# A state-space layer and a SwiGLU block on one core: another order of the 1050 steps behind the first 150, and other engines for some roundings

## The chip, the cores and the metric

The kernel runs on one core of a Trainium2 chip. Its engines work from queues of their own and wait for one another by semaphores: TensorE (PE) multiplies matrices into PSUM, VectorE (DVE), ScalarE (ACT) and GpSimd (POOL) work elementwise, and SyncE (SP) issues most of the DMA transfers. The metric is the device time of one execution in microseconds.

## The reference, cut to what matters

The first half is a chunked scan with a state for each of 4 batches and 8 heads (768 positions, 32 values a head, 16 states), the second an RMS norm and a SwiGLU block on the 3072 rows of 256 that come out of it.

```python
for c in range(nc):
    la = log_a[:, :, sl]
    cum = np.cumsum(la, axis=-1)
    L = np.exp(cum[:, :, :, None] - cum[:, :, None, :]) * causal
    M = np.einsum('bhin,bhjn->bhij', Cc, Bc) * L
    y_intra = np.einsum('bhij,bhjd->bhid', M, xc)
    y_inter = np.einsum('bhin,bhnd->bhid', Cc, state) * np.exp(cum)[:, :, :, None]
    y[:, :, sl] = y_intra + y_inter
    decay_from_j = np.exp(cum[:, :, -1:] - cum)
    Bx = np.einsum('bhjn,bhjd->bhjnd', Bc, xc) * decay_from_j[:, :, :, None, None]
    state = np.exp(np.sum(la, axis=-1))[:, :, None, None] * state + np.sum(Bx, axis=2)
...
xn = x / np.sqrt(np.mean(x * x, axis=-1, keepdims=True) + 1e-06) * rms_g
g = xn @ w_gate
silu = g * (1.0 / (1.0 + np.exp(-g)))
return (silu * (xn @ w_val) @ w_out)
```

## The kernel before

The tokens are worked through in 6 blocks of 512. For each block the scan makes decay matrices L (spread by a DMA, `spread` L653; `subtract` L659; a causal cut L631; an exponential on ACT, L272), products g of C and B (L765), the states' additions A (L830) and the outputs y (L916). From y come the squares (ACT, added by `squares_added` L974 on DVE or POOL), their means ms on PE (L1014), the roots (L272, a load, and a DMA at L1032 and L1039) and the normed rows. The second half of a block has 12 groups f of 128 hidden values, each with a gate and a value product (index m), and 12 output products of two halves.

Large products in float32 are done in three fp32r products of parts: a rounded high part, a low part and a mixed part. So xh, xl, xk stand for the block's rows, wh, wp for the weights, hh, hl, hk for the hidden values. `gv_split` (L1159, step X) is one such product of 6 matmuls; `gv_whole` (L1149, step F) and `products_early` (L1112) are the plain float32 form for block 0. `silu_gv` (L272, ACT) takes the gate product out of PSUM, `hide_gv` (L1174, DVE) multiplies it with the value product into hx, `hid_high` rounds it to hh on ACT (`by_scalar`, L328, step hH) or on DVE (`by_vector`, L331, step hHv), and `hid_part` makes hl on DVE or POOL (L1080, steps hL and hLp) and hk on DVE (L1082). Output products are `product_o` (L1228 in blocks 1 to 4; L1234 for blocks 0 and 5, steps OF and OX) and `product_apart` (L1206, step OY) for the last two quarters of block 5. Results leave by `put` (L1258, L1264) and `put_apart` (L1216).

The weights come in 18 pieces k, fetched by SP (L238, L241, step fetch.k) into a buffer of their own each. ACT (step pow) and DVE (man, wt) turn a piece into float32 values w; wH (ACT) or wHv (DVE) make the high part, wL and wM (L322, DVE) the two others.

Two functions of ACT need different tables: silu, and the set with exponentials and logarithms. `functions` (L264 and L266) issues a table load wherever the next function in the order needs the other table.

What sets the order is a string of 1200 steps, written out by hand: each step calls one of the functions above, and so issues its instructions on each engine and on SP behind those of the steps ahead of it. An engine executes its own share in that order. Buffers are taken first-free from rings in the order of the steps: eight PSUM banks, 29 buffers of 512 float32 for parts and hidden values, and some others.

Of the kernel before, what the change touches and what calls it, by code (L numbers as in the profile page):

```python
# [50 lines left out]
def kernel(  # L51
# [1264 lines left out]
    def token_out():  # L1316
# [92 lines left out]
        i:fetch.9 i:fetch.7 i:fetch.14 b:F.0.4.0 p:S.3 b:xHv.0.1 i:wt.12 p:yi.2 i:man.10 p:ya.2
        p:yi.3 b:silu.0.5 i:man.8 i:wt.10 p:ya.3 i:pow.7 i:man.7 b:silu.0.4 i:hid.0 p:qc.4  # L1410
        p:spread.11 i:wHv.3 i:fetch.15 i:wt.7 i:pow.8 b:F.0.4.1 b:OF.0.1.0 b:silu.0.3 b:sq.1.1
        i:wHv.10 b:yt.1.1 b:xL.0.0 i:wM.3 i:fetch.11 b:yt.1.0 p:spread.10 b:OF.0.0.1 i:wt.8 b:xL.0.1
        b:OF.0.0.0 i:wL.10 i:wM.10 b:xK.0.1 p:spread.9 b:OF.0.1.1 b:sq.1.0 i:wH.7 b:F.0.5.1 i:wL.7
        p:qc.5 i:wM.7 b:X.0.11.0 b:sqa.1 i:wL.3 i:pow.14 b:hid.0.4 b:X.0.7.1 i:wHv.8 i:fetch.13
        b:X.0.2.1 i:man.15 i:wH.5 i:man.14 b:table.5 b:hid.0.7 b:X.0.3.1 b:ms.1 i:fetch.17 p:qb.4
        i:pow.11 i:pow.15 i:wM.8 i:man.11 i:wL.8 b:X.0.6.1 b:rs.1 b:hid.0.3 p:subp.10 b:X.0.9.0
        b:hid.0.5 b:X.0.8.0 i:pow.13 i:wt.11 i:wt.14 b:hid.0.6 i:pow.9 i:man.9 i:wt.15 i:man.13
        i:pow.17 p:sub.9 i:wHv.11 b:hid.0.2 i:wM.11 i:wt.9 i:wL.11 p:vB.4 p:ex.9 b:OF.0.4.0 i:man.17
        i:wH.9 i:wH.15 p:vC.4 b:OF.0.4.1 i:wt.13 b:OF.0.7.1 i:wL.9 i:wH.13 p:spread.8 b:OF.0.5.1
        i:wM.9 p:Tt.4.0 p:subp.11 p:qb.5 p:vC.5 b:rb.1 p:ex.11 b:X.0.10.0 p:x.4 i:wt.17 p:sub.8  # L1420
        b:OF.0.7.0 b:xn.1.1 p:qb.7 b:silu.0.11 p:scale.5 i:wH.4 i:wHv.1 b:xn.1.0 i:wHv.0 b:silu.0.9
        b:X.0.11.1 b:OF.0.5.0 b:xH.1.1 i:wH.17 i:wM.6 p:dT.5 i:wM.0 b:silu.0.8 b:OF.0.2.0 b:OF.0.3.1
        b:xH.1.0 b:xK.1.1 b:silu.0.10 b:X.0.9.1 i:fetch.16 b:OF.0.3.0 i:wL.0 p:dT.4 p:ca.9 b:X.0.8.1
        p:Tt.4.1 b:xL.1.0 p:ex.8 p:Tt.5.1 b:X.0.10.1 b:xK.1.0 i:pow.16 b:xL.1.1 b:exps.1 i:man.16
        b:hid.0.10 p:vB.5 b:OF.0.6.1 b:OF.0.2.1 p:qc.7 b:hid.0.11 b:X.1.0.0 p:ex.10 i:wt.16
        b:OF.0.6.0 p:ca.11 b:X.1.10.0 p:Tt.5.0 b:X.1.10.1 b:OF.0.11.1 i:wL.6 p:x.6 b:hid.0.8 p:qc.6
        b:hid.0.9 p:vB.7 b:silu.1.0 p:Td.4 b:silu.1.10 p:ca.8 b:gb.2 p:dT.6 i:wH.14 b:OF.0.8.1
        i:wM.2 b:X.1.9.0 p:ca.10 p:x.5 b:OF.0.10.1 i:wL.1 b:L.2.2 b:OF.0.9.1 b:L.2.0 b:X.1.8.0
        p:scale.4 i:wH.16 i:wM.15 p:Td.5 b:silu.1.9 p:A.5 b:L.2.3 i:wM.17 p:qc.9 b:L.2.1 p:vC.6
        p:vC.7 p:A.4 p:S.4 p:S.5 i:wH.12 p:Tt.7.1 b:OF.0.9.0 i:wL.17 p:x.7 b:X.1.0.1 b:put.0.1  # L1430
        b:OF.0.8.0 b:hid.1.0 p:yi.4 p:ya.4 p:Tt.6.1 i:wM.1 p:yi.5 p:ya.5 b:hid.1.10 i:wL.12 b:hH.1.0
        i:wM.12 b:silu.1.8 i:wM.4 b:X.1.11.0 b:hH.1.10 b:yt.2.1 b:OF.0.10.0 p:spread.14 p:qb.6
        b:OF.0.11.0 p:scale.7 p:vC.9 i:wL.4 p:scale.6 p:Tt.6.0 b:silu.1.11 b:X.1.1.0 b:table.4
        b:sq.2.1 b:put.0.0 b:hK.1.10 b:X.1.6.0 p:Tt.9.0 b:X.1.11.1 i:wL.15 b:hLp.1.0 i:wM.16
        b:X.1.6.1 b:silu.1.1 b:sq.2.0 b:hK.1.0 b:sqav.2 p:vB.6 p:dT.7 p:spread.12 b:yt.2.0 i:wM.5
        p:spread.13 b:ms.2 b:silu.1.6 i:wM.13 p:A.6 i:wL.16 p:spread.15 p:A.7 p:S.6 b:X.1.5.0
        i:wL.13 b:rs.2 b:hid.1.11 p:Tt.7.0 p:qb.10 i:wL.5 p:scale.9 p:S.7 b:exps.4 b:silu.1.5
        b:X.1.9.1 p:sub.13 b:X.1.1.1 b:X.1.4.0 b:X.1.8.1 b:exps.5 b:rb.2 b:hH.1.11 b:silu.1.4
        p:ex.13 p:Td.6 b:X.1.2.0 b:hid.1.1 b:hid.1.6 b:hK.1.11 p:sub.15 p:sub.14 b:xn.2.1 b:X.1.4.1
        b:X.1.3.0 b:hL.1.11 p:Tt.9.1 b:X.1.5.1 b:silu.1.2 b:hL.1.10 b:X.1.2.1 b:OX.1.0.1 p:subp.12  # L1440
        b:hid.1.4 b:silu.1.3 p:ex.14 b:hid.1.9 p:Td.7 b:hid.1.8 i:wM.14 b:OX.1.11.1 b:hid.1.5
        p:ex.12 b:hH.1.8 p:qb.9 p:ex.15 b:gb.3 p:qc.11 p:cav.14 b:OX.1.11.0 p:ca.15 p:qc.8 b:hid.1.2
        b:hH.1.1 p:cav.12 p:cav.13 b:OX.1.10.1 b:xn.2.0 b:L.3.2 b:OX.1.0.0 b:OX.1.10.0 b:L.3.1
        b:hH.1.6 b:X.1.7.0 b:hLp.1.8 b:L.3.3 b:silu.1.7 p:yi.6 b:L.3.0 b:hK.1.8 p:ya.6 b:xH.2.1
        b:X.1.7.1 b:xH.2.0 b:OX.1.8.0 i:wL.14 b:X.1.3.1 b:hHv.1.4 p:yi.7 p:ya.7 p:vB.9 b:xK.2.0
        b:hK.1.1 b:xL.2.0 b:xL.2.1 b:hid.1.3 b:hH.1.2 b:hLp.1.1 b:xK.2.1 b:hLp.1.4 b:hid.1.7
        b:yt.3.0 b:hK.1.4 b:OX.1.8.1 b:hHv.1.9 b:hLp.1.6 b:X.2.2.0 b:hH.1.7 b:OX.1.1.0 p:spread.16
        b:sq.3.1 b:OX.1.4.1 b:hK.1.9 b:OX.1.4.0 b:sq.3.0 p:spread.18 p:vC.8 b:OX.1.1.1 p:x.9
        b:yt.3.1 p:dT.8 b:hL.1.2 b:hLp.1.7 b:X.2.9.0 b:sqav.3 b:hL.1.9 p:qb.8 b:X.2.0.1 b:hK.1.7
        b:X.2.2.1 b:silu.2.2 p:Tt.8.0 b:silu.2.9 p:sub.16 p:scale.11 p:vB.8 b:X.2.11.0 b:OX.1.7.0  # L1450
        p:sub.18 b:OX.1.7.1 p:x.8 b:hH.1.3 b:hK.1.2 p:scale.8 b:OX.1.9.0 b:ms.3 p:A.8 b:OX.1.2.0
        b:hK.1.3 p:S.8 b:hid.2.2 p:spread.17 b:hL.1.3 p:vC.11 p:ex.16 p:subp.17 b:X.2.7.0 b:X.2.5.0
        b:silu.2.11 b:hHv.1.5 p:Tt.8.1 p:Td.8 b:hK.1.6 p:cav.16 p:spread.19 b:X.2.0.0 b:hL.1.5
        b:X.2.5.1 b:silu.2.0 b:OX.1.9.1 b:silu.2.5 p:vB.10 p:qc.10 b:OX.1.3.1 b:hid.2.5 b:rs.3
        p:dT.11 p:qb.11 b:hH.2.5 b:hid.2.0 p:ex.17 p:ex.18 b:X.2.8.0 p:subp.19 b:hK.1.5 p:ca.18
        p:Tt.11.1 b:X.2.11.1 p:dT.9 b:OX.1.6.1 b:hLp.2.5 p:ex.19 b:X.2.4.0 b:rb.3 b:OX.1.6.0
# [98 lines left out]
```

## Time and profile before

| | us |
|---|---|
| three runs | 364.86, 364.84, 364.15 (median 364.84) |
| profiled execution | 364.29 |
| its span in the trace | 362.5 |
| PE busy | 356.3 |
| DVE busy | 275.3 |
| ACT busy | 183.9, with 28 table loads of 1.283 |
| POOL busy | 74.8 |
| TensorE clock granted | 1.00 |

PE, DVE, ACT and POOL are the engines, PEld is the loading of weights into PE, which overlaps its matmuls. A float32 matmul of the program shows as two records in the trace, one with fp32r operands as one. A row of the chain or the timeline begins with the start and the duration in us; in brackets stands how long the engine had been idle ahead of it, and what released it. "issue" is time in which an engine waited for nothing that the profile shows.

### The profile page before, as it was taken

The page shows a single profiled execution, that of the slowest core. Times are in us where ns is not written, and L with a number is a line of the kernel's source. Part 1 is how long each engine was busy: PE and PEld are TensorE (multiplying, and loading weights), DVE is VectorE, ACT ScalarE, POOL GpSimd, SP SyncE. Part 2 cuts the span into 40 slices and gives each one's busy share as a digit, 9 for nine tenths or more (in the row PEclk, how much of TensorE's full clock was granted, in tenths as well). Part 3 has the DMA queues.
Part 4 walks back from the last instruction along what each step waited for, and adds up shares of the span by engine and source line. Part 5 has one row for each costly group of instructions (what it writes and reads, how often), then busy time and mean ns, then how long its engine had stood idle before and what let it go on. Part 6 is the DMA issues. An engine that isn't in the chain of part 4 may idle for free.

```text
span 362.5 us, 8200 instructions
## 1 busy us (share of the span) xinstructions
PE 356.3 (98%) x3301; PEld 284.0 (78%) x3301; DVE 275.3 (76%) x514; ACT 183.9 (51%) x323; POOL 74.8 (21%) x79
## 2 busy tenths in 40 slices
PE   8999989999999999999999999999999999999996
PEld 5667467888787888788788788788788888888886
DVE  6899998999999999872787884696457446629591
ACT  3879878697288946563236755225811121231110
POOL 4022004124011036212102626010010000511140
PEclk9999999999999999999999999999999999999999
DMA  8889968367525224423302031200101000100004
GB/s 103 187 140 288 272 193 224 107 151 117 103 85 137 44 40 103 103 54 85 60 12 81 7 88 31 45 0 4 36 0 31 1 0 2 29 0 2 0 7 110
DMA packets 94702, 27.95 MB, mean 77 GB/s; under 512 B 77545, under 2 KB 92617, under 8 KB 94665
## 3 DMA queue, kind: packets, MB, share of 16 engines
q1 hardware_dynamic: 92584, 27.30, 32.8%
q8 instruction: 26, 0.43, 0.5%
q10 hardware_dynamic: 2080, 0.13, 0.4%
q14 instruction: 12, 0.09, 0.1%
HBM read 23.68 MB, written 3.74 MB: 76 GB/s over the span
## 4 chain that ended last, share of the span: by engine, by line
PE 95%; DVE 2%; issue 1%; POOL 1%; ACT 0%; POOLq 0%; DVEq 0%
PE gv L1159 50%; PE o L1228 18%; PE o L1234 7%; PE gv L1149 4%; PE y L916 3%; PE o L1206 2%; PE gv L1112 2%; PE g L765 2%; PE A L830 1%; PE g L758 1%; PE y L891 1%; PE e L609 1%; POOL hl L1080 1%; PE ms L1014 0%; DVE hk L1082 0%
## 5 line engine op out<-in xcount | busy, mean ns | idle before, releaser
L1159 PE MATMUL gv<-xh,wh 128*128 128x512 f32 x264 | 84.8, 402 | 0.0
L1159 PE MATMUL gv<-xl,wp 128*128 128x512 f32 x264 | 81.5, 390 | 0.0
L1159 PE MATMUL gv<-xk,wp 128*128 128x512 f32 x264 | 81.4, 389 | 0.0
L272 ACT ACTIVATE hx<-gv 128x512 f32<-128x512 f32 x70 | 40.1, 595 | 75.3 <-PE gv L1159 36.5
L1080 POOL TENSOR_TENSOR hl<-hx,hh 128x512 fp32r<-128x512 f32 x27 | 39.5, 1473 | 172.4 <-PE o L1228 105.8
L1174 DVE SCALAR_TENSOR_TENSOR hx<-gv,hx 128x512 f32<-128x512 f32 x70 | 46.6, 683 | 26.9 <-PE gv L1159 19.3
L1159 PEld LDWEIGHTS gv<-xl,wp 128*128 128x128 f32 x264 | 49.6, 188 | 10.6
L1159 PEld LDWEIGHTS gv<-xk,wp 128*128 128x128 f32 x264 | 49.6, 188 | 10.6
L1159 PEld LDWEIGHTS gv<-xh,wh 128*128 128x128 f32 x264 | 48.6, 188 | 10.5 <-issue 0.6
L1082 DVE SCALAR_TENSOR_TENSOR hk<-hx,hh 128x512 fp32r<-128x512 f32 x60 | 47.1, 792 | 8.9 <-PE o L1228 6.0
L328 ACT ACTIVATE hh<-hx 128x512 fp32r<-128x512 f32 x35 | 21.8, 629 | 43.2 <-PE o L1228 20.3
L1228 PE MATMUL o<-hh,wh 128*128 128x512 f32 x96 | 38.0, 396 | 0.0
L1228 PE MATMUL o<-hl,wp 128*128 128x512 f32 x96 | 37.4, 390 | 0.0
L1228 PE MATMUL o<-hk,wp 128*128 128x512 f32 x96 | 37.4, 389 | 0.0
L1080 DVE TENSOR_TENSOR hl<-hx,hh 128x512 fp32r<-128x512 f32 x33 | 24.1, 744 | 5.3 <-PE o L1228 3.7
L631 POOL TENSOR_SCALAR_AFFINE_SELECT L<-L 64x512 f32<-64x512 f32 (+1 forms) x22 | 18.7, 851 | 45.8 <-ACT L L272 45.0
L322 DVE SCALAR_TENSOR_TENSOR wp<-wh,w 128x512 fp32r<-128x512 f32 x36 | 26.3, 756 | 1.0 <-ACT wh L328 1.0
L1234 PE MATMUL o<-w,hx 128*128 128x256 f32 x96 | 23.0, 381 | 0.0
L1228 PEld LDWEIGHTS o<-hh,wh 128*128 128x128 f32 x96 | 18.0, 188 | 4.3 <-issue 0.4
L1228 PEld LDWEIGHTS o<-hk,wp 128*128 128x128 f32 x96 | 18.0, 188 | 3.8
L1228 PEld LDWEIGHTS o<-hl,wp 128*128 128x128 f32 x96 | 18.0, 188 | 3.5
L1234 PEld LDWEIGHTS o<-w,hx 128*128 128x128 f32 x96 | 18.0, 189 | 3.4 <-issue 0.4
(180 smaller groups left out, 504.3 us busy)
## 6 DMA issues: line engine op xcount, KB each, us to landing
L<-rowd SPq DMA_DIRECT2D x32, 128.0 KB
x<-in_x_dram SPq DMA_DIRECT2D x24, 128.0 KB
...
```

Of the source, the lines that this page charges most:

```text
L272: nc.scalar.activation(**operands)
L322: nc.vector.scalar_tensor_tensor(out=(low_parts, mixed_parts)[i][k], in0=high_parts[k], scalar=(-UP, GAIN)[i], in1=view(ws[k], shape), op0 ...
L328: nc.scalar.activation(out=out, in_=in_, func=AF.Copy, scale=scale)
L631: nc.gpsimd.affine_select(out=L[r], in_=L[r], pattern=[[0, L.shape[1]], [1, HC]], compare_op=ALU.is_ge, fill=0.0, base=0, channel_multipli ...
L916: nc.tensor.matmul(out=o[first:first + n, (p % 2 * 2 + i) * HC:(p % 2 * 2 + i + 1) * HC], start=not groups & opened, stop=True, skip_group ...
L1080: engine.tensor_tensor(out=out, in0=v, in1=high, op=ALU.subtract)
L1082: nc.vector.scalar_tensor_tensor(out=out, in0=v, scalar=REST, in1=high, op0=ALU.mult, op1=ALU.subtract)
L1149: nc.tensor.matmul(out=o, lhsT=view(ws[k], fetched[k][2])[:, t, f % 2 * P:][:, 0:P], rhs=xn[:, t], start=(t == 0), stop=(t == 1))
L1159: nc.tensor.matmul(out=o, lhsT=weights_of(m, t, f)[part], rhs=view(x, [P, TB], F32R), start=(part == t == 0), stop=(part == 2 and t == 1))
L1174: nc.vector.scalar_tensor_tensor(out=v, in0=o, scalar=gain(blk, f), in1=v, op0=ALU.mult, op1=ALU.mult)
L1228: nc.tensor.matmul(out=o, lhsT=w[:, b * P:(b + 1) * P], rhs=v, start=opens, stop=True, skip_group_check=True)
L1234: nc.tensor.matmul(out=o[:, j * DM:(j + 1) * DM], lhsT=v[:, tk], rhs=w, start=opens, stop=True, skip_group_check=True)
```

## The change

Only the string of steps differs. Its first 150 steps and the number of steps are the same; behind them every piece of the string is in another order. A few steps are exchanged for others that do the same on another engine: of the hidden values' roundings hH goes from 35 to 29 and hHv from 25 to 31; of their low parts hL from 33 to 28 and hLp from 27 to 32; of the weights' high parts wH from 10 to 15 and wHv from 8 to 3; of the rows' high parts xH from 9 to 8 and xHv from 3 to 4; of the subtractions, those on DVE from 9 to 6 and those on POOL from 7 to 10; the additions of squares on DVE from 4 to 0 and on POOL from 1 to 5. Table loads follow from the order: 28 before, 38 now. PE's matmuls are the same in number and kind.

```diff
-        i:early.1.0 i:norm.0 p:Tt.2.0 p:T.3 p:Tt.3.1 i:wHv.2 b:xH.0.0 i:man.5 p:Tt.3.0 i:wL.2
...
+        i:early.1.0 i:norm.0 p:Tt.2.0 p:T.3 p:Tt.3.1 i:wHv.2 i:fetch.14 p:Tt.3.0 i:ca.2 p:scale.2
...
-        b:OY.2.0 b:put.4.1 b:OY.1.0 b:putv.5.0 b:puta.1 b:putva.0
...
+        b:put.4.1 b:putv.5.0 b:OY.2.1 b:OY.1.1 b:putva.0 b:puta.1
```

*The first block's outputs (35 to 50 us of the trace before).* PE's rows at that place, of the change against before; g, A and y are the scan's small products, L1112 and L1149 block 0's gate and value products.

```order
+L1112 MATMUL gv<-yt,w 128x256 x8
 L1149 MATMUL gv<-xn,w 128x512 x2
-L1112 MATMUL gv<-yt,w 128x256 x4
 L765 MATMUL g<-T 64x128 x32
 L1149 MATMUL gv<-xn,w 128x512 x6
 L830 MATMUL A<-x,Bd 32x64 x28
-L1149 MATMUL gv<-xn,w 128x512 x4
+L1149 MATMUL gv<-xn,w 128x512 x6
 L916 MATMUL y<-T,S 64x64 x16
 L916 MATMUL y<-L,x 32x64 x32
 L916 MATMUL y<-T,S 64x64 x12
```

Behind A now stand six L1149 matmuls ahead of the y group, where four stood; a group of four L1112 matmuls stands ahead of g, where it stood behind the first two L1149.

SP's transfers at the same time, first before, then with the change (wr are weight pieces, bc and bq rows of B and C, L the spread decays).

```order
L241 DMA wr_720<-in_moe_w_gate_dram 128x2x1023
L241 DMA wr_810<-in_moe_w_val_dram 128x2x1023
L241 DMA wr_812<-in_moe_w_val_dram 128x2x1023
L238 DMA wr_814<-in_moe_w_out_dram 128x2x1023
L173 DMA bc_944<-in_B_dram 128x8x16 x2
L186 DMA bc_944<-in_C_dram 128x1x128 x2
L653 DMA L_949<-rowd_98 64x512 x2
L238 DMA wr_954<-in_moe_w_out_dram 128x2x1023
L241 DMA wr_982<-in_moe_w_val_dram 128x2x1023
```

```order
L238 DMA wr_653<-in_moe_w_out_dram 128x2x1023
L241 DMA wr_717<-in_moe_w_val_dram 128x2x1023
L238 DMA wr_719<-in_moe_w_out_dram 128x2x1023
L241 DMA wr_721<-in_moe_w_val_dram 128x2x1023
L241 DMA wr_742<-in_moe_w_gate_dram 128x2x1023
L238 DMA wr_801<-in_moe_w_out_dram 128x2x1023
L241 DMA wr_925<-in_moe_w_val_dram 128x2x1023
L238 DMA wr_987<-in_moe_w_out_dram 128x2x1023
L653 DMA L_997<-rowd_98 64x512 x4
```

Eight weight pieces stand one behind the other where four stood; the rows of B and C, and the spreads, come behind them.

*The end of the program.* POOL's last instructions, before and with the change (the numbers are those of buffers' contents, so hl_4347 is the low part that is made from hx_4079).

```order
L1080 TENSOR_TENSOR hl_4161<-hx_3929,hh_4148 128x512
L1080 TENSOR_TENSOR hl_4220<-hx_3864,hh_4154 128x512
L1080 TENSOR_TENSOR hl_4300<-hx_4159,hh_4289 128x512
L1080 TENSOR_TENSOR hl_4317<-hx_4211,hh_4259 128x512
L1080 TENSOR_TENSOR hl_4347<-hx_4079,hh_4330 128x512
```

```order
L1080 TENSOR_TENSOR hl_4180<-hx_3990,hh_4084 128x512
L1080 TENSOR_TENSOR hl_4241<-hx_4093,hh_4218 128x512
L1080 TENSOR_TENSOR hl_4279<-hx_4016,hh_4239 128x512
L1080 TENSOR_TENSOR hl_4298<-hx_3906,hh_4151 128x512
L1080 TENSOR_TENSOR hl_4353<-hx_4293,hh_4300 128x512
```

PE's rows that wait for such parts, before and with the change (L1234 and L1206 are output products of block 5).

```order
L1234 MATMUL o_4095<-wh14_1390,hh_4289 128x256
L1234 MATMUL o_4095<-wp_1927,hl_4300 128x256
L1234 MATMUL o_4095<-wp_1927,hk_4308 128x256
L1234 MATMUL o_4095<-wh14_1390,hh_4289 128x256
L1234 MATMUL o_4095<-wp_1927,hl_4300 128x256
L1234 MATMUL o_4095<-wp_1927,hk_4308 128x256
L1206 MATMUL o_4102<-wh17_1224,hh_4259 128x256
L1206 MATMUL o_4102<-wp_1446,hl_4317 128x256
L1206 MATMUL o_4102<-wp_1446,hk_4277 128x256
```

```order
L1206 MATMUL o_4124<-wh14_1268,hh_4239 128x256
L1206 MATMUL o_4124<-wp_1683,hl_4279 128x256
L1206 MATMUL o_4124<-wp_1683,hk_4304 128x256
L1206 MATMUL o_4124<-wh13_1352,hh_4229 128x256
L1206 MATMUL o_4124<-wp_1588,hl_4326 128x256
L1206 MATMUL o_4124<-wp_1588,hk_4281 128x256
L1234 MATMUL o_4117<-wh12_1100,hh_4300 128x256
L1234 MATMUL o_4117<-wp_1187,hl_4353 128x256
L1234 MATMUL o_4117<-wp_1187,hk_4339 128x256
```

Before, PE takes hl_4300 and hl_4317 within these nine matmuls and hl_4347 another 25 behind them, all three of POOL's last instructions. Now hl_4353 alone is POOL's last, and what PE reads ahead of it here (hl_4328, hl_4279, hl_4326) it has had before.

*The middle, 145 to 175 us.* ACT's rows, before and with the change (L264 loads the table with silu, L266 the one with exponentials; hx<-gv is a silu, L<-L an exponential).

```order
L995 COPY yt<-y 64x4x64 x2
L272 ACTIVATE hx<-gv 128x512
L328 ACTIVATE T<-T,tmask 128x256
L272 ACTIVATE hx<-gv 128x512
L328 ACTIVATE hh<-hx 128x512
L266 ACT_TABLE_LOAD
L272 ACTIVATE L<-L 128x512
L264 ACT_TABLE_LOAD
L272 ACTIVATE hx<-gv 128x512
L328 ACTIVATE T<-T,tmask 128x256
L272 ACTIVATE hx<-gv 128x512 x2
L266 ACT_TABLE_LOAD
```

```order
L266 ACT_TABLE_LOAD
L272 ACTIVATE L<-L 128x512
L264 ACT_TABLE_LOAD
L272 ACTIVATE hx<-gv 128x512 x3
L266 ACT_TABLE_LOAD
L272 ACTIVATE L<-L 128x512 x2
L328 ACTIVATE T<-T,tmask 128x256
L264 ACT_TABLE_LOAD
L272 ACTIVATE hx<-gv 128x512
L266 ACT_TABLE_LOAD
L272 ACTIVATE roots<-ms,eps 128x128
L272 ACTIVATE roots<-roots 128x128
```

Before, three table loads stand in twelve rows, now five, and each silu of the stretch stands between two of them.

More of the change, by code (lines that the diff above doesn't have):

```diff
@@ L1409 @@
[L1409 to L1456, printed above, removed]
@@ new lines @@
+        b:silu.0.4 p:ya.3 b:sq.1.1 b:sq.1.0 i:wt.8 i:pow.11 i:pow.10 b:OF.0.0.0 i:wt.14 b:xK.0.1
+        i:wt.7 b:OF.0.0.1 b:F.0.5.1 i:fetch.17 i:hid.1 i:wH.7 b:OF.0.1.1 i:man.10 b:hid.0.4
+        p:spread.8 p:spread.10 p:qb.4 b:sqa.1 b:xL.0.0 b:ms.1 p:spread.9 b:xL.0.1 p:spread.11
+        b:yt.1.0 b:OF.0.1.0 b:OF.0.4.0 i:wH.8 i:wL.3 i:man.11 b:yt.1.1 i:fetch.13 b:rs.1 i:wt.10
+        b:X.0.3.1 i:wL.7 i:wM.7 b:X.0.2.1 i:gains i:wL.8 b:hid.0.5 i:wt.11 p:qb.7 i:wH.11 i:wL.6
+        b:X.0.6.1 i:man.15 i:man.9 b:X.0.7.1 i:wM.8 i:wH.10 i:pow.15 i:pow.9 i:wH.12 p:qc.5
```

168 lines of the change are left out of this document (105 added, 63 removed).

## The prediction

> **What bounds the kernel now.** The page comes first: busy time by engine, the slices, and the chain that ended last.
>
> ```profile
> PE 356.3 (98%) x3301; PEld 284.0 (78%) x3301; DVE 275.3 (76%) x514; ACT 183.9 (51%) x323; POOL 74.8 (21%) x79
> ...
> PE 95%; DVE 2%; issue 1%; POOL 1%; ACT 0%; POOLq 0%; DVEq 0%
> ```
>
> PE is busy for 98% of the span, and 95% of the chain is PE itself. "issue" and POOL hold 1% each, so only a few microseconds are waits. The view by stretches of time says where they can lie (columns: span of the stretch, then PE, PEld, DVE, ACT, POOL busy, granted clock, DMA share).
>
> ```profile
> 40.00:60.00 20.00, 18.70 (x292) 12.20 (x291) 18.54 (x41) 16.43 (x31) 1.51 (x2) 1.00 0.82 226
> 60.00:80.00 20.00, 20.00 (x96) 16.47 (x96) 20.00 (x34) 16.54 (x28) 6.12 (x6) 1.00 0.55 153
> 140.00:160.00 20.00, 20.00 (x118) 16.12 (x117) 18.20 (x32) 11.85 (x23) 4.86 (x4) 1.00 0.45 101
> 160.00:180.00 20.00, 20.00 (x148) 16.33 (x147) 9.29 (x17) 8.28 (x15) 5.15 (x6) 1.00 0.37 80
> 300.00:345.00 45.00, 45.00 (x223) 38.21 (x223) 27.43 (x44) 9.28 (x17) 8.96 (x7) 1.00 0.04 7
> ```
>
> From 60 to 345 us PE has no gap and the clock is 1.00; what DVE, ACT and POOL do there costs nothing as long as it is in time. The change issues the same matmuls, so it can win only at the gaps of 40 to 60 us and behind 345 us, and lose anywhere that an operand comes late. In 60 to 80 us DVE has no idle time at all: there a loss is nearest.
>
> **First gap.** The timeline of PE (start, length, operation):
>
> ```profile
> 40.90 0.79 PE L830 MATMUL A<-x,Bd 64*32 64x64 f32 x56
> 41.62 3.70 PE L1149 MATMUL gv<-xn,w 128*128 128x512 f32 x8
> 45.25 0.49 PE L916 MATMUL y<-T,S 32*64 32x64 f32 x32
> 45.67 0.79 PE L916 MATMUL y<-L,x 64*32 64x64 f32 x57
> 47.76 0.31 PE L916 MATMUL y<-L,x 64*32 64x64 f32 x7 [1.30 <-issue]
> ```
>
> PE stops for 1.30 us inside one group of y matmuls, on no engine and no semaphore. The next rows are the DMA view of two windows (the packets of 37 to 45.2 us, where the view lists no instruction queue; the packets of 45.2 to 46.2, and the instruction queue there):
>
> ```profile
> DMA packets 3214, 2.32 MB, mean 282 GB/s; under 512 B 2147, under 2 KB 3214, under 8 KB 3214
> ...
> DMA packets 200, 0.39 MB, mean 393 GB/s; under 512 B 15, under 2 KB 199, under 8 KB 199
> ...
> q8 instruction: 1, 0.02, 5.5%
> ```
>
> The instruction queue q8 moves nothing in the first window and one packet of 0.02 MB in the second, beside 393 GB/s of traffic. I read the gap as PE out of instructions: the packet began some 45.2 us, PE went on at 47.76, 2.5 us later. It was probably asked for in the group A at 40.9 us, some four microseconds earlier, and stood behind the weights on the DMA engines. That is inferred from the times; no row shows the request.
>
> The Trainium skill speaks against this reading: by "Runtime: NRT & Kernel Launch", section "Instruction fetch mechanics", an engine prefetches its instructions in order in blocks of 16 KiB and the cost of crossing a block is "mostly hidden". The size agrees with the packet of 0.02 MB, the hiding doesn't agree with a 1.30 us gap that names no other releaser; by the rule this gap would have another cause and nothing of the first term below would come.
>
> **Last gap.** From the chain and the timelines of POOL and PE:
>
> ```profile
> 349.04 5.21 POOL L1080 TENSOR_TENSOR hl<-hx,hh 128x512 fp32r<-128x512 f32 x3 [10.02 <-PE o L1228]
> ...
> 350.81 1.75 POOL hl L1080
> ...
> 351.99 0.28 PE L1206 MATMUL o<-wh,hh 128*128 128x256 f32 x1
> 352.60 0.39 PE L1206 MATMUL o<-wp,hl 128*128 128x256 f32 x1 [0.33 <-POOL hl L1080]
> 352.82 0.28 PE L1206 MATMUL o<-wp,hk 128*128 128x256 f32 x1
> 352.94 0.29 PE L1206 MATMUL o<-wh,hh 128*128 128x256 f32 x1
> ```
>
> POOL forms three low parts hl one behind the other in 5.21 us. The second ends at 352.56 (350.81 + 1.75), and PE, which starts one such matmul each 0.12 us (352.82 to 352.94), starts there after 0.61 us and the next after 0.22: it loses 0.49 + 0.10 = **0.6 us**. Behind the last matmul stand one copy and the store, in both kernels.
>
> **The change, part by part.** The sum starts from the profiled execution, 364.29 us (span 362.5 and 1.8 around it). The runs shown have the median 364.84, with one at 364.15; so the profiled one lies 0.55 below their median and inside their spread.
>
> *Order at 40 us.* The y group now stands behind six L1149 matmuls, before behind four, with the same group A ahead. Four of these are eight records of 3.70 us in the timeline, so PE reaches the stopping instruction 1.85 us later, at about 46.46 + 1.85 = 48.3 us. If the packet comes as before, PE could go on from 47.76: nothing is left to wait for and **1.3** goes. SP, however, now issues eight weight loads in a row where it issued four. One such load (128 × 2 × 1023 elements of two bytes, 0.52 MB) takes 1.9 us at the 282 GB/s above. If the packet stands behind one more of them, PE goes on at 49.6 and 1.3 us of waiting stay; behind two, 3.2 us stay, which is 1.9 more than now. If the four ahead of the packet are the same, as their issue ahead of it suggests, nothing stays. I take −1.0, nearer to the lower end since the first four loads keep their places, with the ends −1.3 and +1.9. The following packet is asked for while y runs, with the loads still going, but the instructions that it brings start some 40 matmul and weight-load instructions behind y, about 5 us of PE: within this allowance.
>
> *The tail.* The last POOL low part is now formed from the product that ends 93 rows ahead of its use, at 0.12 us a row 11 us, against 58 rows (7.0) before; the two in the middle are DVE's. The tightest chain that I find there is DVE's: a silu, then hx, three hk, a transpose of the output and an hl. At the 0.744 of an hl on DVE for each of the six (row below) and 0.60 for the silu that is 5.1 us, for 72 rows or 8.6 us. So **−0.6**, and next in line is nothing within 3 us. Ends −0.6 and, if POOL is late once more, 0.
>
> *One visit fewer.* The small matmuls of another type (y, A, g, ms) stand in one group less behind 30 us. What one group costs around itself, from the chain:
>
> ```profile
> 31.04 1.72 PE gv L1149 x4
> ...
> 49.25 1.91 PE gv L1149 x4
> ```
>
> The same four records take 1.91 behind y and 1.72 in a stream: **−0.2** for one group less, between 0 and −0.4 (both its edges).
>
> *Engines exchanged.* Costs, from the page and the groups by line (busy, mean ns):
>
> ```profile
> L1080 POOL TENSOR_TENSOR hl<-hx,hh 128x512 fp32r<-128x512 f32 x27 | 39.5, 1473 | 172.4 <-PE o L1228 105.8 <-PE o L1234 18.8 <-ACT hh L328 13.6
> L1080 DVE TENSOR_TENSOR hl<-hx,hh 128x512 fp32r<-128x512 f32 x33 | 24.1, 744 | 5.3 <-PE o L1228 3.7 <-POOL hl L1080 1.2
> L328 ACT ACTIVATE hh<-hx 128x512 fp32r<-128x512 f32 x35 | 21.8, 629 | 43.2 <-PE o L1228 20.3 <-DVE hx L1174 10.6 <-DVE hk L1082 6.4
> L331 DVE TENSOR_SCALAR hh<-hx 128x512 fp32r<-128x512 f32 x25 | 11.5, 468 | 8.1 <-PE o L1228 3.7 <-PE o L1234 3.4 <-PE gv L1159 0.5
> L264 ACT ACT_TABLE_LOAD x14 | 18.0, 1283 | 0.2
> ```
>
> Five hl go from DVE to POOL (+7.4 us there, −3.7 on DVE) and six hh from ACT to DVE (−3.8, +2.8); four squares and three subtractions go from DVE to POOL and five weight roundings from DVE to ACT. DVE has less to do and POOL and ACT more, and PE, which has no gap there, gains nothing by it: 0, covered by PE's own stream. Without that cover the price is on ACT: its table loads rise from 28 to 38, 10 × 1.283 = 12.8 us. They are dear where they bunch: by PE time 145 to 171 us ACT has ten loads where it had four, and its work there grows from 15.4 to about 21.8 us of 25.4 (ten loads 12.8, seven silu at 0.60, four exponentials, the rest). What a switch costs around itself:
>
> ```profile
> 146.42 1.28 ACT L266 ACT_TABLE_LOAD   x1
> 147.71 0.63 ACT L272 ACTIVATE L<-L 128x512 f32<-128x512 f32 x1
> 148.36 1.28 ACT L264 ACT_TABLE_LOAD   x1
> 150.26 0.60 ACT L272 ACTIVATE hx<-gv 128x512 f32<-128x512 f32 x1 [0.62 <-PE o L1228]
> 156.71 1.09 ACT L272 ACTIVATE hx<-gv 128x512 f32<-128x512 f32 x2 [5.46 <-PE gv L1159]
> ```
>
> A load follows an activation within 0.02 us (147.71 + 0.63, then 148.36), so a pair of switches with one exponential between holds a silu up by 1.28 + 0.63 + 1.28 = 3.2 us. ACT had 5.46 us to spare ahead of 156.71, and PE never waited for it here. I add **+0.3** for new short waits, between 0 and 3.8 (the slower case below).
>
> The Trainium skill, "ScalarE: Activation LUTs", section "What ACT_TABLE_LOAD costs", has 1283 ns for the load, as here, and a drain of about 1380 ns besides, and advises to batch the calls by table. The rows show no drain; by that price ten more loads would be 26.6 us and the stretch above would hold some 36 us of work in 25.4, ten too many. It is a form of the slower rival, and weighs little since two rows contradict it.
>
> Sum: 364.29 − 1.0 − 0.6 − 0.2 + 0.3 = **362.8 us**, 2.0 below the median of the runs shown.
>
> **The rivals.** *No change:* the first gap stays, since the packet is held up by the longer row of weight loads or since it has another cause, and one short wait appears: 364.29 − 0.8 + 0 to +1.0, that is 363.5 to 364.5. For it: 0.82 of the DMA is taken in 40 to 60 us as it is. Against: y comes 1.85 us later whatever its cause, and a wait for a fixed time shrinks. *Slower, by ACT at 145 to 171 us:* pairs of table loads stand ahead of silu, whose results hx, hh, hl and hk PE needs for its next output group and whose PSUM bank the next product needs. It decides when a silu comes more than about 3 us late, the pair's own length; if three pairs each come through with the 1.28 us of one load, it costs 3.8: 364.29 − 1.5 + 3.8 = 366.6; if one does, 364.1. For it: 86% load (21.8 of 25.4) with waits among its steps. Against: 8.28 of 20 us busy behind it, so it catches up. *No gap, all early:* the first wait goes in full and nothing new comes, 364.29 − 1.3 − 0.6 − 0.4 = 362.0. *The change does nothing at its places* because the gaps move rather than go: 364.3, part of the first rival.
>
> **How the numbers follow.** A measurement of this kernel can tell about 0.2% or 0.73 us from no change. Forecast, 362.0 to 363.6 with the early case: 0.57. No change, 363.5 to 364.8: 0.21. Slower by ACT or by two weight loads ahead of the packet, 365 to 367: 0.22. The range 361.9 to 365.7 reaches above into the slower case until about two in ten are left out. Faster than 364.1 has the forecast and a little of the second case, less the little of the forecast that fails: 0.58; within 0.2% 0.20; slower 0.22.
>
> **What will show it.** In the changed profile: the bracket "issue" at the y matmuls at 48 us below 0.5 us; no POOL hl as releaser of L1206 or L1234 behind 340 us; PE 20.00 busy in each stretch of 20 us from 60 to 340; 38 table loads and ACT about 18 us of 20 in the fullest stretch, without PE waiting. Wrong would be: an "issue" of over 1 us again, or one that is new at 50 to 55 us (the second packet); PE waiting for ACT's or DVE's parts in 60 to 110 or 145 to 175 us; PE below 20.00 in any stretch there by over 0.5 us.

## The result, and the profile after

The changed kernel takes 366.56 us (median of 6 runs, 366.07 to 367.12), the kernel before 364.23 (median of 6): a ratio of 1.0061 with a 95% interval of 1.0047 to 1.0075. Forecast were 362.8 us and a gain; it is a loss of 2.3 us. The profiled execution of the changed kernel has a span of 364.5 us, 2.0 more than before.

The page's busy times and chain, of the changed kernel:

```profile
PE 357.9 (98%) x3301; PEld 283.6 (78%) x3301; DVE 280.9 (77%) x504; ACT 195.7 (54%) x331; POOL 91.7 (25%) x91
...
PE 76%; DVE 17%; issue 3%; SPq 1%; ACT 1%; DMA 1%; POOL 0%; DVEq 0%; POOLq 0%; ACTq 0%
```

DVE executes ten instructions fewer than before (504 against 514), and five fewer of its hl, yet it is busy 5.6 us longer (280.9 against 275.3). The chain, nearly all PE before, now runs 17% on DVE. Both point to the same engine. Most of the longer time is in one group, the hk, before and then with the change:

```profile
L1082 DVE SCALAR_TENSOR_TENSOR hk<-hx,hh 128x512 fp32r<-128x512 f32 x60 | 47.1, 792 | 8.9 <-PE o L1228 6.0
...
L1082 DVE SCALAR_TENSOR_TENSOR hk<-hx,hh 128x512 fp32r<-128x512 f32 x60 | 51.9, 878 | 16.7 <-PE o L1228 8.9
```

The same sixty instructions take 4.8 us more. The view of what PE waits for, and two stretches of the view by time (same columns as in the prediction):

```profile
PE o L1228 <- DVE hl L1080: 1.2, 1, 1.2
PE idle L434 <- DVE warm L476: 1.1, 1, 1.1
PE o L1234 <- DVE hl L1080: 0.5, 1, 0.5
PE gv L1159 <- DVE wp L322: 0.3, 1, 0.3
...
60.00:80.00 20.00, 19.66 (x87) 15.73 (x86) 20.00 (x33) 16.17 (x24) 2.48 (x2) 1.00 0.41 79
...
120.00:140.00 20.00, 18.79 (x252) 14.33 (x250) 19.66 (x31) 9.78 (x15) 5.80 (x5) 1.00 0.28 56
```

The "issue" gap and the wait for POOL are gone from the list; three waits for DVE's parts are new, at 65, 131 and 354 us. (The wait at L434 is the program's start.) At 65 and 131 us PE had no gap before. PE at the y group of block 1, which stopped for 1.30 us before:

```profile
47.37 0.86 PE L916 MATMUL y<-L,x 64*32 64x64 f32 x64
48.16 0.46 PE L916 MATMUL y<-T,S 32*64 32x64 f32 x24
```

No stop is left there. Now the largest new one, at 131 us: DVE's, POOL's and PE's timelines side by side.

```profile
127.54 0.69 DVE L1082 SCALAR_TENSOR_TENSOR hk<-hx,hh 128x512 fp32r<-128x512 f32 x1
128.14 1.76 DVE L646 TENSOR_TENSOR L<-L,limit 128x512 f32<-128x512 f32 x1
129.83 0.68 DVE L1082 SCALAR_TENSOR_TENSOR hk<-hx,hh 128x512 fp32r<-128x512 f32 x1
...
132.03 0.68 DVE L1080 TENSOR_TENSOR hl<-hx,hh 128x512 fp32r<-128x512 f32 x1
...
128.09 1.27 POOL L1080 TENSOR_TENSOR hl<-hx,hh 128x512 fp32r<-128x512 f32 x1 [5.21 <-PE o L1228]
...
131.18 0.39 PE L1228 MATMUL o<-hh,wh 128*128 128x512 f32 x1
132.76 0.50 PE L1228 MATMUL o<-hl,wp 128*128 128x512 f32 x1 [1.19 <-DVE hl L1080]
```

The L646 instruction takes 1.76 us. Its twin at 126.0 us takes 0.69. POOL begins an hl at 128.09, DVE its instruction at 128.14, POOL ends at 129.36 and DVE at 129.90, 0.54 us later: it looks as if DVE did most of its work only when POOL was done. Everything behind it in DVE's queue is 1.07 us late, and DVE has no idle time to make it up. The hl that PE needs is ready at 132.71 and PE, due at 131.41, stops: 1.58 us from one matmul to the next, where 0.23 is normal, so 1.35 are lost.

The same picture stands at the other two, and at a smaller stop of 139.6 to 141 us. At 65 us two POOL subtractions (59.76 to 62.49) lie over two mantissa steps of DVE, and the weights' part behind them is late; at 139.6 and at 354 us a POOL hl lies over an hk:

```profile
59.76 2.73 POOL L659 TENSOR_TENSOR L<-L,tok 128x512 f32<-128x512 f32 x2 [0.54 <-DMA L<-rowd]
...
60.32 2.45 DVE L300 TENSOR_SCALAR w<-wr 128x512 f32<-128x512 uint32 x2
...
65.82 0.50 PE L1159 MATMUL gv<-xl,wp 128*128 128x512 f32 x1 [0.34 <-DVE wp L322]
...
137.92 1.46 POOL L1080 TENSOR_TENSOR hl<-hx,hh 128x512 fp32r<-128x512 f32 x1 [2.81 <-PE o L1228]
...
138.14 1.78 DVE L1082 SCALAR_TENSOR_TENSOR hk<-hx,hh 128x512 fp32r<-128x512 f32 x1
...
351.34 1.53 POOL L1080 TENSOR_TENSOR hl<-hx,hh 128x512 fp32r<-128x512 f32 x1 [0.87 <-ACT hh L328]
...
351.63 1.78 DVE L1082 SCALAR_TENSOR_TENSOR hk<-hx,hh 128x512 fp32r<-128x512 f32 x1
...
353.90 0.28 PE L1234 MATMUL o<-wh,hh 128*128 128x256 f32 x1
354.67 0.39 PE L1234 MATMUL o<-wp,hl 128*128 128x256 f32 x1 [0.49 <-DVE hl L1080]
```

An overlap alone is no loss. Before the change two POOL subtractions ran at nearly the same time, 59.76 to 62.26 us, with a mantissa step of 1.26 us beside them, and PE was full: what is held must also be needed at once.

Not every DVE instruction is long when POOL works. The views of single lines of the changed kernel give least, median and most nanoseconds:

```profile
L646 DVE TENSOR_TENSOR L<-L,limit x7: 667/693/1762, 25.6 to 226.8; 128x512 f32<-128x512 f32 x6, 128x1024 f32<-128x1024 f32 x1
...
L1082 DVE SCALAR_TENSOR_TENSOR hk<-hx,hh x60: 665/686/1783, 103.9 to 355.1; 128x512 fp32r<-128x512 f32 x60
...
L1174 DVE SCALAR_TENSOR_TENSOR hx<-gv,hx x70: 654/684/731, 52.9 to 349.8; 128x512 f32<-128x512 f32 x70
L788 DVE TENSOR_TENSOR L<-g,L x20: 678/682/703, 35.7 to 241.2; 128x512 f32<-128x512 f32 x20
L300 DVE TENSOR_SCALAR w<-wr x18: 401/420/1264, 21.1 to 71.8; 128x512 f32<-128x512 uint32 x18
...
133.81 1.30 POOL L1080 TENSOR_TENSOR hl<-hx,hh 128x512 fp32r<-128x512 f32 x1 [4.45 <-PE o L1228]
...
134.42 0.68 DVE L1174 SCALAR_TENSOR_TENSOR hx<-gv,hx 128x512 f32<-128x512 f32 x1
```

hk and L646 read two tiles of SBUF and reach 1.78 us. Of all 72 instructions of L1082 (hk and xk), the 14 that begin with at least 0.3 us of a POOL instruction still to run take 0.98 to 1.78 us, the other 58 at most 0.71. hx at L1174 and L at L788 do the same kind of arithmetic on as many elements, but one of their inputs is PSUM: in 90 instructions none goes above 0.73, though 21 of them begin while a POOL instruction runs, as the hx at 134.42 does. The Trainium skill states this in "SBUF — State Buffer", section "SBUF: two separate sides": DVE and GpSimd share one pair of ports, a DVE instruction with two SBUF inputs and a GpSimd instruction that reads SBUF exclude each other, and the one that comes second blocks for the whole of the first. The rows agree nearly, with a hold of 1.07 us against the 1.22 us that POOL's instruction still had to run. The mantissa step L300 has one input only and is long beside POOL all the same (1.26 against 0.42), so having two inputs is not the only condition.

The distances from each matmul to the next, over the median of their kind before, add up to the whole difference. A stop is measured in this way from here on, where no bracket is named. Stops of the changed kernel behind 60 us: 1.0 at 63 to 66 us, 1.46 at 131, 0.5 at 139 to 141, 1.0 at 350 to 355 and 0.3 in small ones, 4.3 together (each with the about 0.1 that the matmul behind a stop is slower). Before: 1.5 at 46, 0.6 at 352 and 0.2 at 56, 2.3. The difference is 2.0 us, as the spans have it.

### The profile page after: what moved, and what is told of

It is laid out like the page before. It is cut to its first block, busy times and chain, and to the rows that moved or that the text cites. A ratio compares the mean times of both kernels' runs of the same rounds, so it can differ in the third digit from the quotient of the medians.

```text
span 364.5 us, 8227 instructions
## 1 busy us (share of the span) xinstructions
PE 357.9 (98%) x3301; PEld 283.6 (78%) x3301; DVE 280.9 (77%) x504; ACT 195.7 (54%) x331; POOL 91.7 (25%) x91
## 4 chain that ended last, share of the span: by engine, by line
PE 76%; DVE 17%; issue 3%; SPq 1%; ACT 1%; DMA 1%; POOL 0%; DVEq 0%; POOLq 0%; ACTq 0%
PE gv L1159 42%; PE o L1228 17%; PE o L1234 5%; DVE wp L322 3%; PE y L916 3%; DVE hk L1082 2%; DVE hx L1174 2%; PE o L1206 2%; DVE S L859 2%; DVE w L306 1%; PE g L758 1%; PE g L765 1%; DMA x<-in_x_dram 1%; DVE w L300 1%; DVE hl L1080 1%
## 5 line engine op out<-in xcount | busy, mean ns | idle before, releaser
L1080 POOL TENSOR_TENSOR hl<-hx,hh 128x512 fp32r<-128x512 f32 x32 | 45.9, 1439 | 139.3 <-PE o L1228 76.6
L1174 DVE SCALAR_TENSOR_TENSOR hx<-gv,hx 128x512 f32<-128x512 f32 x70 | 46.6, 685 | 27.0 <-PE gv L1159 23.1
L1082 DVE SCALAR_TENSOR_TENSOR hk<-hx,hh 128x512 fp32r<-128x512 f32 x60 | 51.9, 878 | 16.7 <-PE o L1228 8.9
L1228 PE MATMUL o<-hl,wp 128*128 128x512 f32 x96 | 37.7, 393 | 1.2 <-DVE hl L1080 1.2
L1228 PE MATMUL o<-hh,wh 128*128 128x512 f32 x96 | 38.3, 399 | 0.0
L1228 PE MATMUL o<-hk,wp 128*128 128x512 f32 x96 | 37.6, 391 | 0.0
L328 ACT ACTIVATE hh<-hx 128x512 fp32r<-128x512 f32 x29 | 17.7, 629 | 35.0 <-PE o L1228 13.4
L1080 DVE TENSOR_TENSOR hl<-hx,hh 128x512 fp32r<-128x512 f32 x28 | 20.1, 722 | 10.5 <-PE o L1228 9.4
L1234 PE MATMUL o<-w,hx 128*128 128x256 f32 x96 | 23.2, 383 | 0.0
L1228 PEld LDWEIGHTS o<-hl,wp 128*128 128x128 f32 x96 | 18.1, 188 | 5.2 <-DVE hl L1080 1.9
L974 POOL TENSOR_TENSOR sq<-sq 128x512 f32<-128x512 f32 x5 | 7.7, 1546 | 53.9 <-ACT sq L272 50.7
```

The source lines that it names most:

```text
L328: nc.scalar.activation(out=out, in_=in_, func=AF.Copy, scale=scale)
L1080: engine.tensor_tensor(out=out, in0=v, in1=high, op=ALU.subtract)
L1082: nc.vector.scalar_tensor_tensor(out=out, in0=v, scalar=REST, in1=high, op0=ALU.mult, op1=ALU.subtract)
L1174: nc.vector.scalar_tensor_tensor(out=v, in0=o, scalar=gain(blk, f), in1=v, op0=ALU.mult, op1=ALU.mult)
L1228: nc.tensor.matmul(out=o, lhsT=w[:, b * P:(b + 1) * P], rhs=v, start=opens, stop=True, skip_group_check=True)
L1234: nc.tensor.matmul(out=o[:, j * DM:(j + 1) * DM], lhsT=v[:, tk], rhs=w, start=opens, stop=True, skip_group_check=True)
```

## The experiments

Three theories: **A**, POOL's instructions hold DVE's, and a full DVE queue passes the delay on to PE; **B**, the new order as such puts some parts too late in DVE's queue, without POOL; **C**, the forecast's slower rival, ACT's ten additional table loads. Each ratio is to the kernel before, run on the same chip. There it took 364.8 to 364.95 us, against 364.23 beside the changed kernel, so kernels of different chips are best compared by their ratios (the changed kernel's is 1.0061).

### e1: six low parts made by ACT

```diff
-        b:hLp.1.6 ... b:hLp.1.9 ... b:hLp.5.11 ... b:hLp.5.4 ... b:hLp.5.10 ... b:hLp.5.1
+        b:hLc.1.6 ... b:hLc.1.9 ... b:hLc.5.11 ... b:hLc.5.4 ... b:hLc.5.10 ... b:hLc.5.1
...
+    def hid_copied(blk, f):
+        hl[blk, f] = b = h.take(2 + (blk == NBLK - 1), "hl")
+        by_scalar(view(b, [P, TB], F32R), view(hx[blk, f], [P, TB]), BELOW)
```

> The changed kernel, but six low parts hl that POOL made by subtraction (hidden groups 6 and 9 of block 1, groups 1, 4, 10 and 11 of block 5) are made by ACT as a copy of hx instead, so the numbers of these parts are left out. Same order of steps, same buffers, same matmuls. Theory A (a DVE instruction that starts while POOL works is held until POOL's ends, and DVE's queue behind it is late for PE): the DVE subtraction at L646 that took 1.76 us at 128.1 us takes 0.7, the hk of 1.78 at 138 and in the last 20 us take 0.7, and PE's stops at 131.2 us (1.35), 139.6 to 141 (0.5) and 353.9 (0.65) shrink to 0 to 0.4 each; time 2.0 to 2.7 below the changed kernel's 366.6, that is 363.9 to 364.6. Theory B (the new order simply puts hl too late in DVE's queue, POOL has no part in it): the stops stay at 1.0 us or more at 131 and 0.4 or more at 354, time 366.2 to 366.6. Theory C (ACT's additional table loads make the parts late): six more ACT instructions of 0.63 us make it 366.6 or more.

364.33 us, ratio to before 0.9988 (0.9975 to 1.0001): 2.2 below the changed kernel by the medians, 2.7 by the ratios. The busy times, the stretch of 120 to 140 us and that of the end:

```profile
PE 357.3 (99%) x3301; PEld 284.2 (78%) x3301; DVE 274.6 (76%) x504; ACT 198.5 (55%) x337; POOL 83.7 (23%) x85
...
120.00:140.00 20.00, 20.00 (x314) 15.68 (x315) 18.97 (x33) 11.77 (x18) 3.08 (x3) 1.00 0.28 56
345.00:363.00 18.00, 14.29 (x117) 13.96 (x115) 8.51 (x15) 3.69 (x7) 0.00 (x0) 1.00 0.26 59
```

DVE executes the same 504 instructions as in the changed kernel and is busy 6.3 us less (274.6 against 280.9). PE is full again in 120 to 140 us. The three places that the expectation names, 131, 139.6 and 354 us, have no stop left, with the order unchanged and ACT given more to do: B and C fall, as causes of these stops. The 2.0 to 2.7 of A are met. Two stops for instructions, 0.5 us at 48.7 and 0.47 at 104, stand in this execution in their place. The stop at 65 us is gone too, but its subtractions are still POOL's and lie over DVE's; PE comes there 1.3 us later, so e1 shows nothing about that stop.

### e9: only one hold taken away

Six edits at once could hide what each does, so here is one alone.

```diff
-b:hLp.1.6
+b:hLc.1.6
```

> The changed kernel with one instruction other: the hl of block 1, group 6 (POOL at 128.1 us) is an ACT copy of hx, so the numbers of that part are left out; all else as changed. Theory A: the L646 instruction beside it takes 0.7 instead of 1.76 us, the hl on DVE three steps behind ends 1.07 us earlier, and PE's stop of 1.35 us at 131.2 shrinks to 0.2 to 0.4; nothing else moves, time 365.3 to 365.7. Theory B (order): stop unchanged, 366.6.

365.44 us, ratio 1.0030 (1.0016 to 1.0044). The rows that stood above, of this kernel (its lines behind the new function are numbered 6 higher, so L1234 is the L1228 of the others):

```profile
128.19 0.69 DVE L646 TENSOR_TENSOR L<-L,limit 128x512 f32<-128x512 f32 x1
...
131.00 0.68 DVE L1080 TENSOR_TENSOR hl<-hx,hh 128x512 fp32r<-128x512 f32 x1
...
131.25 0.39 PE L1234 MATMUL o<-hh,wh 128*128 128x512 f32 x1
131.73 0.50 PE L1234 MATMUL o<-hl,wp 128*128 128x512 f32 x1
```

L646 takes 0.69 instead of 1.76, hl begins at 131.00 instead of 132.03, and the distance between the two matmuls falls from 1.58 to 0.48 us. That is 1.10 us, and the kernel is 1.1 us faster than the changed one by the medians and by the ratios (both intervals are about 0.5 us to either side). That is A, in one place, with a single instruction taken from POOL.

### e10: the useless pair of table loads left out

```diff
-b:exps.4
```

> The changed kernel without the step that loads the exponentials' table at 124.1 us and so has the other loaded again at 125.4 us, with no exponential between them: two table loads fewer, 2.57 us of ACT just ahead of three silu and of the stop at 131 us. Theory C (ACT's table loads make the parts late): the silu at 126.7 come 2.5 us earlier, the stop of 1.35 us goes, 365.2. Theory A (DVE is held by POOL and full): DVE has no idle time there, so the stop stays within 0.3 us, 366.3 to 366.7.

366.49 us, ratio 1.0052 (1.0034 to 1.0069): no gain. ACT, DVE and PE of this kernel:

```profile
124.98 1.09 ACT L272 ACTIVATE hx<-gv 128x512 f32<-128x512 f32 x2 [0.88 <-DVE wp L322]
...
128.13 1.77 DVE L646 TENSOR_TENSOR L<-L,limit 128x512 f32<-128x512 f32 x1
...
132.75 0.50 PE L1228 MATMUL o<-hl,wp 128*128 128x512 f32 x1 [1.21 <-DVE hl L1080]
```

The silu come 1.7 us earlier (124.98; 126.71 before this edit), and nothing else moves. C has no part in this stop. In the stretch that the rival named, 145 to 171 us, PE has no stop at all in the changed kernel:

```profile
145.00:171.00 26.00, 26.00 (x144) 21.11 (x143) 19.83 (x35) 21.38 (x27) 7.78 (x6) 1.00 0.33 69
```

### e5: the same six low parts given to DVE

```diff
-        b:hLp.1.6 ... b:hLp.1.9 ... b:hLp.5.11 ... b:hLp.5.4 ... b:hLp.5.10 ... b:hLp.5.1
+        b:hL.1.6 ... b:hL.1.9 ... b:hL.5.11 ... b:hL.5.4 ... b:hL.5.10 ... b:hL.5.1
```

> The changed kernel with the same six hl as in e1 given back to DVE as subtractions (nothing left out). DVE then has six instructions of 0.68 us more and POOL six fewer. Theory A (a POOL instruction holds a DVE instruction that reads two tiles of SBUF, 1.07 us in the row at 128.1 us and as much at 138 and at 347 to 353): each exchange gives DVE 1.07 back for 0.68, so the stops at 131, 139 and 354 us shrink by 0.4 for each hold ahead of them, about 0.4, 0.3 and 0.7; time 365.0 to 366.0, below the changed kernel's 366.6. Theory B (DVE has too much to do at these places, POOL doesn't matter): DVE is 0.68 later for each, the stops grow by 0.7 or more, time 367.5 to 369.

365.48 us, ratio 1.0024 (1.0010 to 1.0039), as expected. DVE has six instructions more, and the kernel is 1.1 us faster than the changed one (1.3 by the ratios); the stop at 131 us loses 0.5 us and that at 354 is gone. Where DVE's queue is full, an hl on POOL costs DVE more (1.07) than the hl itself on DVE (0.60 from one start to the next). "Given back" is right for three of the six only: 1.6, 5.4 and 5.11 are POOL's in the kernel before as well.

### e6 and e7: order and engines taken apart

Each step in the order of the one kernel on the engines of the other. The expectations count 46 exchanges; the two strings differ in 88 steps, 18 hl from DVE to POOL and 13 from POOL to DVE among them.

```diff
-        b:xHv.0.0 ... i:wH.1 ... p:subp.9 ... b:sqa.2 ... b:hLp.1.10
+        b:xH.0.0 ... i:wHv.1 ... p:sub.9 ... b:sqav.2 ... b:hL.1.10
```

> The changed order with all 46 engine exchanges undone (each step on the engine that it has in the kernel before). Theory A: POOL's busy time falls from 92 to about 76 us, the holds with it; of the stops behind 60 us (4.2 us) about half go, since the order was laid out for the other engines, time 364.3 to 365.8. Rival (the order alone is slower): no gain or a loss, 366.2 to 368.

> The kernel before with the 46 engine exchanges of the change made in its own order. Theory A: POOL's busy time rises from 75 to about 92 us, hk's mean on DVE from 792 to over 850 ns, PE stops for DVE parts appear; time 0.7 to 3 above 364.2, that is 365 to 367. Rival (the order alone is slower): the time stays at 364.0 to 364.6.

e6 takes 373.02 us, ratio 1.0233 (1.0201 to 1.0264); e7 375.68, ratio 1.0303 (1.0269 to 1.0337). Both are far slower than either kernel, and both expectations fall. In e7 hk on DVE goes to a mean of 938 ns from 792, as A has it, but PE's waits there are for POOL's hl (2.1 us), L788 (2.0) and xl (1.4). In e6 POOL is busy 74.3 us, no more than before the change, and PE waits for other parts of DVE and 1.6 us for ACT; yet hk has a mean of 914 ns there, more than in the changed kernel (878). So it is not POOL's total that lengthens hk: which DVE instruction the order lays beside which POOL instruction counts too. Order and engines fit one another in both kernels; how much of the loss belongs to the one or the other as a whole can't be told from these two.

### e2, e12 and e3: the y group by itself

e2 and e12 are one kernel: the kernel before, with one step moved. e3 is the changed kernel with the reverse.

```diff
 p:S.3 b:xHv.0.1 i:wt.12 p:yi.2
+b:F.0.4.1 ahead of p:yi.2
-b:F.0.4.1 behind i:pow.8
```

> The kernel before with one step moved: the third L1149 product of block 0 that stood right behind the first y group now stands ahead of it, so that y comes 0.9 us x 2 later, as in the changed kernel. Theory of the instruction fetch (PE runs out of instructions, the packet was asked for some four microseconds earlier and comes by the clock, not by PE's place): the issue gap of 1.30 us at 46.46 us is gone or below 0.2, time 1.2 to 1.5 below 364.2, about 362.8. Rival (the gap belongs to the y group itself): the gap moves with y and keeps its 1.3 us, time 364.2.

> The kernel of e2 once more (the kernel before, y behind six L1149 matmuls as in the change), in more rounds, since e8, which has the same step moved and one hl in the last 20 us on another engine, came out no faster than the kernel before. If the instruction packet decides, the gap at y is 0.3 to 0.7 us instead of 1.3 and the time 0.7 to 1.2 below the kernel before on the same chip; if e2 was a favourable chip, the time is within 0.4 of it.

> The changed kernel with the reverse of it: one L1149 product moved from ahead of the y group to behind it, so that y comes 1.8 us earlier, with the eight weight loads in a row left as they are. Theory of the instruction fetch: an issue gap of 1.0 to 1.5 us comes back inside y at about 46.5 us, PE goes on at 47.7 us as in the kernel before, time up to 1.4 above 366.6. Rival (the longer row of weight loads sets when the packet comes): PE goes on at 49 us or later, gap of 2.5 us or more. Rival (the gap was no fetch): none.

e2 takes 363.70 us, ratio 0.9977 (0.9956 to 0.9998), e12 363.79, ratio 0.9978 (0.9963 to 0.9994). e3, executed once, takes 369.21. PE in e2, then in e3:

```profile
47.37 0.76 PE L916 MATMUL y<-L,x 64*32 64x64 f32 x53
48.58 0.33 PE L916 MATMUL y<-L,x 64*32 64x64 f32 x11 [0.45 <-issue]
...
46.51 0.79 PE L916 MATMUL y<-L,x 64*32 64x64 f32 x57
48.91 0.31 PE L916 MATMUL y<-L,x 64*32 64x64 f32 x7 [1.61 <-issue]
```

A matmul of y or L1149 is two of these records. With four records more ahead of y, PE stops four records sooner inside it, behind 53 instead of 57. Counted from the start, PE stops behind its 598th matmul record in the kernel before, in e2 and in e3: the stop stands at one place of the program and does not move with y. When it ends is told by the instruction queue q8. Its one packet near this place, of 16,384 bytes, starts at 45.27 us (before), 46.14 (e2) and 46.43 (e3), and PE goes on 2.49, 2.44 and 2.48 us later. In the changed kernel the packet starts at 45.22 and PE comes to the place at 47.89, 2.67 us later, so there is nothing to wait for; in e12's profiled execution it is 45.61 and 48.02. So the gap is PE out of instructions, and it is what is left between PE's arrival and the packet. The packet does not come at a fixed time: in e2 it starts 0.87 us later than before, though PE was at the same matmuls at 41 us, and 0.45 us of the gap stay (bracket), where the expectation had 0.2 at most. e3's expectation missed as well (PE going on at 47.7, at most 368.0 us); its rival, the eight weight loads, had PE going on at 49 us or later with a gap of 2.5, which is not seen either (48.91 and 1.61). What delays the packet is not shown.

In e2 as in e12 the gain, 1.1 us of medians, is somewhat below the 1.2 to 1.5 that e2's expectation gave, since a part of the gap stayed in e2's trace. e12's profiled execution was its slowest (367.72 us) and has a wait of 1.9 us for ACT's roots; it doesn't stand for the median.

### e4, e8 and e11: three attempts at a faster kernel

```diff
e4, on the changed kernel:
-p:subp.10 ... p:subp.11 ... b:hLp.1.9 ... b:exps.4
+p:sub.10 ... p:sub.11 ... b:hL.1.9
+b:hL.1.2 ahead of p:cav.13, b:put.4.0 behind b:hL.5.5
e8, on e2:
-b:hLp.5.11
+b:hL.5.11
e11, on e5:
-b:hHv.1.6 ... b:exps.4 ... b:hHv.1.5 ... b:xHv.2.0
+b:hH.1.6 ... b:hH.1.5 ... b:xH.2.0
```

> The changed kernel with its late DVE places mended: hl of block 1, group 2 moved ahead of the L646 step that was held (it stood six DVE steps behind), the transpose of the output moved behind the two last hl on DVE, two subtractions (groups 10 and 11 of L659) and one hl (block 1, group 9) given from POOL back to DVE, and one pair of table loads without a use left out. Theory A with the stops as they were measured in the changed kernel (63 to 66 us 1.0, 131 us 1.46, 139.6 us 0.5, 354 us 0.75): most of these 3.7 us go, time 363.0 to 363.8, below the kernel before. Rival (DVE is short of time as such from 60 to 135 us, and a step moved ahead makes another late): the stops come back within 5 us of the same places, time 365 to 366.6.

> The kernel before with the step of e2 moved, and in the last 20 us the middle one of POOL's three hl (block 5, group 11) given to DVE. The gap at the y group goes from 1.30 to 0.45 or less as in e2, and PE's stop of 0.6 us at 352 for POOL's hl goes: time 363.0 to 363.4, the fastest so far. If POOL's instruction holds the new DVE hl so that it is late as well, half of the 0.6 stays and it is 363.5.

> The changed kernel as in e5 (six hl from POOL back to DVE), and three high parts of 0.42 us near the stops of 126 to 144 us given from DVE to ACT (hh of block 1, groups 5 and 6, and xh of block 2), with the useless pair of table loads left out so that ACT has room. Nothing of the computation is left out. By theory A DVE is then 0.85 us earlier at 132 than in e5, and the stop of 0.83 us there goes; those at 126 (0.34) and 144 (0.38) get smaller; 65 (0.5) stays. Time 364.0 to 364.7, about that of the kernel before. If another step of DVE takes the place, 365.2 to 365.8.

None came as far as it should. e4 takes 366.50 us, ratio 1.0033 (1.0013 to 1.0052), 1.0 us below the changed kernel by the ratios: the stops at 65, 131, 139 and 354 us are gone, but others of about 0.4 to 0.6 us stand at 91, 103 (for instructions), 134 (for the L788 that hl had been moved past) and 143 us. The mantissa steps at 60 us, with the two subtractions no longer POOL's, are short, 0.77 for two instead of 2.45. The moved transpose costs too; that row, and SP's output transfers in e4, then in the changed kernel:

```profile
60.38 0.77 DVE L300 TENSOR_SCALAR w<-wr 128x512 f32<-128x512 uint32 x2
...
354.73 5.76 SPq L1260 DMA_DIRECT2D out_dram<-ob  x8
...
361.60 0.91 SPq L1218 DMA_DIRECT2D out_dram<-ob  x2
...
354.07 5.06 SPq L1260 DMA_DIRECT2D out_dram<-ob  x8
...
361.17 0.93 SPq L1218 DMA_DIRECT2D out_dram<-ob  x2
```

SP needs over 5 us for eight output transfers, and the last stores stand behind them: e4's last matmul starts 1.1 us earlier than that of the changed kernel, its last store is issued 0.4 later. The rival of the expectation was right in its time, and in part in its places (134 and 143 us). e11 takes 366.22, ratio 1.0034 (1.0020 to 1.0047), above both times of its expectation: the stop at 131 us is gone, but there are 1.1 us at 63 to 66, 0.4 at 145 and a stop for instructions at 104 us (0.7). e8 takes 364.99, ratio 1.0006 (0.9989 to 1.0022), 1.3 more than e2, though its stop at 352 us fell from 0.6 to 0.2. Its profiled execution, at 366.89 us far above its median, had a late DMA at 41 us (0.9) and stops at 58 to 63 us that e2's had not; why it lost what e2 had won stays open. The fastest kernel of the study is that of e2 and e12, 0.2% below the kernel before in two sets of runs.

## Why the prediction was wrong, point by point

- **The first gap, −1.0 (down to −1.3):** right, and larger (1.5 with the slower matmul behind it). The reading as a lack of instructions is borne out: PE stops at the same record in three kernels and goes on 2.44 to 2.49 us behind the packet. The "mostly hidden" that the prediction quotes from the Trainium skill, "Runtime: NRT & Kernel Launch", section "Instruction fetch mechanics", doesn't hold for this place. That all of it went is partly luck: the packet was taken to come as before, and in e2 it came 0.87 us later.
- **The tail, −0.6:** wrong in its second half; it came out as +0.4. The wait for POOL's hl went, as said; but "the tightest chain" was put at 5.1 us for 8.6, with each of its six DVE instructions at 0.744 us and DVE free for them. Four POOL instructions lie over DVE's in 344 to 353 us, three of its hk take 1.78 (one is quoted), and PE lost 1.0 us there, against 0.6 before.
- **One visit fewer, −0.2:** no run shows it by itself; the groups are 18 against 19, as counted.
- **Engines exchanged, 0:** the step that failed. The forecast said "DVE has less to do and POOL and ACT more, and PE, which has no gap there, gains nothing by it: 0, covered by PE's own stream", and looked for the price on ACT. It has no term for POOL holding DVE. DVE had less to do and took longer, 280.9 us instead of 275.3, 4.8 of it in hk. The forecast also counted the exchanges net and gave the new order behind 60 us no more than the +0.3 below; but it is order and engines together that lay POOL's instructions over others of DVE. At 131 and at 65 us the POOL steps (hLp.1.6, subp.10 and subp.11) are POOL's in both kernels, and only their neighbours are new; at 139.6 us and for the last hl at 354 the steps were moved to POOL (hLp.1.9, hLp.5.1). The forecast itself had the row that names the place, 20.00 us busy of 20 on DVE at 60 to 80 us ("there a loss is nearest"), and the hk had a mean of 792 and a median of 684 ns before the change. It didn't ask what makes that mean.
- **New short waits, +0.3:** mis-sized with it. They are 3.2 us behind 60 us and ahead of 345, and nearly all are DVE's.
- **The slower rival** had the right total, 366.6, for the wrong cause: ACT carried its table loads (e10), and PE was full from 145 to 171 us, where the rival was placed.

With these terms as measured, 364.29 − 1.5 + 0.4 − 0.2 (a stop at 56 us that went) + 3.2 is 366.2 us, beside 366.33 for the profiled execution. Shown is A for the stop at 131 us (e9), and for 131, 139.6 and 354 us together (e1). For 65 us it rests on e4 alone, where other steps were changed too. How the holds of the other POOL instructions add up to DVE's lateness ahead of these places was not tried one by one.
